# Low parts of four weights: a transfer that adds the weight to its negated upper part, in place of a subtraction on VectorE

## The chip, the cores and the metric

The kernel runs on one core of a Trainium2 chip. The metric is the device time of one execution in microseconds (us). The core's engines have separate instruction queues, each worked off in order: TensorE (PE: matmuls, with PEld its weight loads), VectorE (DVE), ScalarE (ACT), GpSimd (POOL) and SyncE (SP, which here only issues transfers). Each waits for the others by semaphores. Transfers run on 16 DMA engines, whoever issues them.

## The reference

A recurrence over time (4 batches, 8 heads, 768 steps, head size 48) gives the rows x of a gated network:

```
state = alpha[:, :, t, :, None] * state + k[t] (outer) v[t]
y[:, :, t] = q[t] @ state
x = y as 3072 rows of 384
h = x @ w_in            # 384 x 2048
g = h * tanh(log1p(exp(h)))
out = g @ w_out         # 2048 x 384
```

The weights come as 64-bit numbers, everything else as f32.

## The kernel before

**The work.** The recurrence is cut into 24 chunks of 64 steps by 2 pairs of batches; each becomes a few dozen small matmuls on PE (the turned keys, L724; products with the state and scores, L745 to L763; values and the update of the state, L783 to L809), with scans and products on DVE (L672 to L700). A chunk's output is 128 rows of x. The network goes in 100 *units*: a unit takes 2 or 4 chunks (256 or 512 rows) through one of 16 weight blocks f. A unit has an *up* (L1017, nine matmuls into a bank h), a chain on ACT and DVE (L1026, L1029, L1032, L1035 on ACT; the gate, L1044, on DVE; L1051 on ACT for g's upper part; L1054 on DVE for its lower part) and a *down* (L1089, three matmuls for each of its chunks). There are two banks h, so an up waits until the gate has read the bank of the unit two before.

**Two parts for every operand.** A product in full precision is made of three: upper by upper, upper by lower, lower by upper. So each weight block is split into an upper part `ws[:, 0, f]` and a lower part `ws[:, 1, f]`. The first two of every three matmuls use the upper part of the weight, the third the lower part.

**How a weight is made (`weight`, L401 on).** SP loads 768 KB into one of 2 `stage` buffers. DVE puts the bits together in one of 2 `lead` buffers in three steps (L428, L433, L438). ACT writes the upper part (L449). The lower part is `lead` minus the upper part, in one of three ways that the table `W_LOW` names per block: by PE and ACT (L467 to L471), by POOL (L477, two halves) or by DVE (L455):

```
    6: ('DVE', ''), 7: ('POOL', ''), 8: ('POOL', ''), 9: ('DVE', ''), 10: ('DVE', ''), 11: ('POOL', ''),
    12: ('POOL', ''), 13: ('POOL', ''), 14: ('DVE', ''), 15: ('POOL', ''),
```

So DVE makes the low parts of blocks 6, 9, 10 and 14. Below, w6 means block 6; unit n's buffers are t*n* and g*n*. Units 8 to 14 are the first seven wide ones and use w4 to w10 in turn.

**The order.** Every operation is a `Task` with an engine, a cost, a lateness, a due key, the tasks that it needs and the buffers that it uses. `Plan.order` plays these through in a model of the engines and issues them in the order that comes out, so an added or dearer task moves others on all engines. What runs on the chip is that fixed order, with waits for what each instruction needs.

Of the kernel before, what the change touches and what calls it, by code (L numbers as in the profile page):

```python
# [11 lines left out]
F32 = mybir.dt.float32  # L12
# [4 lines left out]
AF = mybir.ActivationFunctionType  # L17
ALU = mybir.AluOpType
# [103 lines left out]
class Plan:  # L122
# [13 lines left out]
    def add(  # L136
        self, engine, cost, late, key, emit, needs=(), uses=(), behind=(), port=False, size=0,
        sends=False, steps=0,
    ):
        t = Task(engine, cost, late, key, emit, port)  # L140
        t.size, t.sends, t.steps = size, t.sends or sends, steps
        t.needs, t.uses, t.behind = list(needs), list(uses), list(behind)
        for u in t.uses:
            u.left += 1
            u.key = min(u.key, key)
        self.tasks.append(t)
        return t
# [131 lines left out]
COST = {  # L279
    "load": (0.45, 2.0), "apart": (0.19, 0.32),  # L280
    "move": (0.63, 2.5), "store": (0.4, 3.0),
    "fill": (0.23, 0.28), "fill0": (0.44, 0.47),
    "off": (0.55, 0.75), "w off": (0.84, 1.08), "lead": (0.47, 0.58), "bits": (0.87, 0.98),
    "w hi": (0.745, 0.88), "w left": (0.42, 0.56), "w lo": (1.05, 1.2), "w lo2": (0.88, 1.0),
    "w check": (0.92, 1.2),
    "scan": (1.16, 1.27), "inverse": (0.09, 0.21), "mult": (0.6, 0.72), "check": (0.2, 0.34),
    "state": (0.48, 0.55), "state0": (0.5, 0.6), "mask": (0.65, 0.8),
# [22 lines left out]
def fast_path(ctx, tc, qka, v, w, out, good):  # L310
    nc = tc.nc
# [64 lines left out]
    add, last_col = plan.add, NSEG * (L + 1)  # L376

    def new(buffer, shape, name, pool=None, dtype=F32):
        buffer.tile = (pool or sb).tile(
            shape, dtype, tag=buffer.tag, name=name, bufs=plan.slots[buffer.tag]  # L380
        )
        return buffer.tile


    def in_bank(bank):
        return sums_at[int(bank.tag[1])] if bank.tag != "h" else h_at[bank.slot]
# [20 lines left out]
    ready_w, checked = {}, []  # L407

    def weight(f):
        key = weight_unit[f] - W_LEAD + W_SHIFT.get(f, 0.0)  # L410
        stage = plan.buffer("stage")

        def load():
            t = new(stage, [P, 2, DM, 2], f"ws{f}", dtype=I32)
            return nc.sync.dma_start(
                t.rearrange("p m c w -> p (m c w)"),
                w[f].rearrange("p m c -> p (m c)").bitcast(I32),
            )

        got = add(  # L420
            "SP", *COST["load"], max(key, FIRST_W + f) - 4, load, uses=[stage], size=786
        )
        lead = plan.buffer("lead")
        words = lambda z: stage.tile[:, :, :, z]

        def begin():
            new(lead, [P, 2, DM], f"w_lead{f}", dtype=I32)
            nc.vector.tensor_scalar(  # L428
                lead.tile, words(1), 3, 0x3FFFFFF8, ALU.logical_shift_left, ALU.bitwise_and
            )  # L430

        def signs():
            nc.vector.scalar_tensor_tensor(  # L433
                lead.tile, words(1), -0x40000000, lead.tile, ALU.bitwise_and, ALU.bitwise_or
            )

        def ends():
            nc.vector.scalar_tensor_tensor(  # L438
                lead.tile, words(0), 29, lead.tile, ALU.logical_shift_right, ALU.bitwise_or
            )  # L440

        bits = add("DVE", *COST["lead"], key, begin, [got], [stage, lead], port=True)
        bits = add("DVE", *COST["bits"], key + 0.01, signs, [bits], [stage, lead], port=True)
        bits = add("DVE", *COST["bits"], key + 0.02, ends, [bits], [stage, lead], port=True)
        both = lambda: lead.tile.bitcast(F32)
        hi, lo = ws[:, 0, f], ws[:, 1, f]

        def upper():
            nc.scalar.activation(hi, both(), AF.Copy)  # L449

        a = add("ACT", *COST["w hi"], key + 0.03, upper, [bits], [lead])
        how, tag = W_LOW[f]
        if how == "DVE":
            def lower():
                nc.vector.tensor_tensor(lo, both(), hi.bitcast(F32), ALU.subtract)  # L455

            b = add("DVE", *COST["w lo2"], key + 0.035, lower, [a], [lead], port=True)
            ready_w[f, 0] = ready_w[f, 1] = [a, b]
            return
        for m in range(2):  # L460
            k = key + 0.5 * m
            if how == "PE":
                bank = plan.buffer(tag)

                def off(bank=bank, m=m):
                    p = in_bank(bank)[:, :DM]
                    nc.tensor.matmul(p, ident, both()[:, m], start=True, stop=False)  # L467
                    nc.tensor.matmul(p, minus_ident, hi[:, m], start=False, stop=True)

                def left(bank=bank, m=m):  # L470
                    nc.scalar.activation(lo[:, m], in_bank(bank)[:, :DM], AF.Copy)  # L471

                t = add("PE", *COST["w off"], k + 0.04, off, [a], [lead, bank], steps=6)
                b = add("ACT", *COST["w left"], k + 0.05, left, [t], [bank])
            else:
                def lower(m=m):
                    nc.gpsimd.tensor_tensor(  # L477
                        lo[:, m], both()[:, m], hi[:, m].bitcast(F32), ALU.subtract
                    )

                b = add("POOL", *COST["w lo"], k + 0.04, lower, [a], [lead], port=True)
            ready_w[f, m] = [a, b]
# [692 lines left out]
    for f in range(NFF):  # L1175
        weight(f)
        weight_check(f)
# [285 lines left out]
```

## Time and profile before

| | |
|---|---|
| median of 3 runs | 498.51 us (498.22 to 499.92) |
| the profiled execution, its own time | 497.71 us |
| its span, first to last instruction | 496.0 us |
| PE busy | 484.6 us (98%) |
| ACT busy | 382.1 us (77%) |
| DVE busy | 323.1 us (65%) |
| POOL busy | 25.3 us (5%) |
| granted TensorE clock | 0.998 of 2.4 GHz |

The page of the profile has the busy time of each engine, the span in 40 slices and the chain of work that ended last. Views of the trace give the instructions in order of time, the waits (who waited for whom) and the transfers. Matmuls are pipelined, so the length of one contains the passage of others; the step from one group's start to the next is the price used below.

### The profile page before, as it was taken

How to read it: one execution, taken by the hardware profiler on the slowest of the kernel's cores; microseconds unless marked ns; L12 is line 12 of the kernel's file. 1: busy time of each engine (PE TensorE's matmuls, PEld its weight loads, DVE VectorE, ACT ScalarE, POOL GpSimd, SP SyncE). 2: the span in 40 equal slices, each digit the busy share in tenths (PEclk: the TensorE clock that was granted, in tenths of full speed). 3: DMA queues.
4: the chain of work that ended last, by engine and by line, in shares of the span. 5: the costliest groups of instructions: out<-in, count | busy, mean ns of one | idle time of the engine just before them, and what ended most of it. 6: DMA issues, size and time to landing. Idle time of an engine off the chain costs nothing.

```text
span 496.0 us, 12822 instructions
## 1 busy us (share of the span) xinstructions
PE 484.6 (98%) x5319; PEld 432.5 (87%) x5319; DVE 323.1 (65%) x522; ACT 382.1 (77%) x864; POOL 25.3 (5%) x27
## 2 busy tenths in 40 slices
PE   6999999999999999999999999999999999999995
PEld 4688889899899989999989899999989899999994
DVE  7999999999973694447867783863474343343333
ACT  3578786886788778857777897889789899997772
POOL 2003201413000000000000000000000000000000
PEclk9999999999999999999999999999999999999999
DMA  7877544606000250115152543603153412100001
GB/s 248 316 285 236 181 151 157 238 35 214 13 0 9 78 172 1 66 59 175 28 213 75 183 164 99 207 24 118 71 171 93 172 41 106 64 1 0 1 0 68
DMA packets 18926, 56.22 MB, mean 113 GB/s; under 512 B 3440, under 2 KB 11312, under 8 KB 18864
## 3 DMA queue, kind: packets, MB, share of 16 engines
q1 hardware_dynamic: 18592, 55.11, 32.5%
q8 instruction: 42, 0.69, 0.6%
q10 hardware_dynamic: 272, 0.26, 0.2%
q14 instruction: 20, 0.16, 0.1%
HBM read 48.87 MB, written 4.72 MB: 108 GB/s over the span
## 4 chain that ended last, share of the span: by engine, by line
PE 85%; DVE 9%; DMA 3%; issue 1%; ACT 1%; SPq 0%; DVEq 0%; ACTq 0%
PE sums_at L1089 39%; PE h_at L1017 37%; PE att_at L790 2%; PE att_at L752 2%; DVE w_lead L433 2%; PE h_at L763 2%; DMA ws<-in_wp_dram 1%; DVE w_lead L438 1%; PE att_at L724 1%; DMA qka<-in_qka_dram 1%; PE h_at L802 1%; DVE w_lead L428 1%; DVE t L1044 1%; DVE g L1054 1%; DVE rest L672 1%
## 5 line engine op out<-in xcount | busy, mean ns | idle before, releaser
L1089 PE MATMUL sums_at<-ws,g 128*128 128x384 f32 x1152 | 223.9, 340 | 0.1
L1017 PE MATMUL h_at<-xs,ws 128*128 128x512 f32 (+1 forms) x900 | 214.2, 384 | 0.2 <-DVE t L1044 0.2
L1089 PEld LDWEIGHTS sums_at<-ws,g 128*128 128x128 f32 x1152 | 202.4, 188 | 8.1 <-ACT ws L471 0.4
L1017 PEld LDWEIGHTS h_at<-xs,ws 128*128 128x128 f32 x900 | 163.3, 188 | 28.4 <-DVE t L1044 0.5
L1054 DVE SCALAR_TENSOR_TENSOR g<-t,g 128x512 fp32r<-128x512 f32 (+1 forms) x100 | 67.8, 679 | 124.2 <-ACT g L1051 123.9
L1026 ACT ACTIVATE t<-h_at 128x512 f32<-128x512 f32 (+1 forms) x100 | 58.0, 580 | 63.6 <-PE h_at L1017 60.8
L1051 ACT ACTIVATE g<-t 128x512 fp32r<-128x512 f32 (+1 forms) x100 | 60.3, 604 | 11.5 <-PE sums_at L1089 5.3
L1029 ACT ACTIVATE t<-t 128x512 f32<-128x512 f32 (+1 forms) x100 | 61.3, 613 | 2.3
L1032 ACT ACTIVATE t<-t 128x512 f32<-128x512 f32 (+1 forms) x100 | 61.2, 612 | 2.2
L1044 DVE SCALAR_TENSOR_TENSOR t<-t,h_at 128x512 f32<-128x512 f32 (+1 forms) x87 | 57.1, 657 | 8.3 <-ACT t L1035 8.2
L1035 ACT ACTIVATE t<-t 128x512 f32<-128x512 f32 (+1 forms) x100 | 60.4, 604 | 0.5
L672 DVE TENSOR_TENSOR_SCAN rest<-qka,behind 112x520 f32<-112x520 f32 x24 | 30.4, 1268 | 0.4 <-DMA qka<-in_qka_dram 0.2
L685 DVE TENSOR_TENSOR_SCAN qka<-qka,ahead 112x520 f32<-112x520 f32 x24 | 30.6, 1274 | 0.0
L477 POOL TENSOR_TENSOR ws<-w_lead,ws 128x384 fp32r<-128x384 f32 x14 | 22.1, 1598 | 98.3 <-ACT ws L449 98.3
L1026 ACT ACTIVATION_READ_ACCUMULATOR t<-h_at 128x1 f32 x100 | 19.4, 194 | 0.0
L1041 DVE COPY held<-h_at 128x512 f32<-128x512 f32 x13 | 9.0, 691 | 15.8 <-ACT t L1026 15.8
L831 ACT ACTIVATE xs<-att_at 112x384 fp32r<-112x384 f32 (+1 forms) x24 | 12.2, 513 | 6.2 <-PE att_at L809 3.4
L695 DVE TENSOR_TENSOR qka<-qka 112x512 f32<-112x512 f32 x24 | 16.4, 684 | 0.1
L681 DVE TENSOR_TENSOR qka<-qka,rest 112x512 f32<-112x512 f32 x24 | 15.8, 659 | 0.0
L433 DVE SCALAR_TENSOR_TENSOR w_lead<-ws,w_lead 128x768 int32<-128x768 int32 x16 | 15.7, 982 | 0.1
L438 DVE SCALAR_TENSOR_TENSOR w_lead<-ws,w_lead 128x768 int32<-128x768 int32 x16 | 15.3, 957 | 0.1
L449 ACT ACTIVATE ws<-w_lead 128x768 fp32r<-128x768 f32 x16 | 13.4, 839 | 2.3 <-DVE w_lead L438 2.2
(100 smaller groups left out, 366.7 us busy)
## 6 DMA issues: line engine op xcount, KB each, us to landing
qka<-in_qka_dram SPq DMA_DIRECT2D x22, 772.5 KB, 5.8
ws<-in_wp_dram SPq DMA_DIRECT2D x16, 768.0 KB, 4.5
wc<-in_wp_dram SPq DMA_DIRECT2D x16, 768.0 KB, 4.5
v<-in_vp_dram SPq DMA_DIRECT2D x24, 192.0 KB, 4.5
out_dram<-osb SPq DMA_DIRECT2D x15, 192.0 KB, 2.6
xs<-x SPq DMA_DIRECT2D x104, 16.0 KB, 1.8
out_dram<-part SPq DMA_DIRECT2D x8, 192.0 KB, 2.6
qka<-in_qka_dram SPq DMA_DIRECT2D x2, 260.5 KB, 4.4
```

The lines of the kernel that those rows point to most:

```text
L433: nc.vector.scalar_tensor_tensor(lead.tile, words(1), -0x40000000, lead.tile, ALU.bitwise_and, ALU.bitwise_or)
L672: nc.vector.tensor_tensor_scan(t[:, :0:-1], alpha()[:, :0:-1], behind[:, ::-1], 0.0, ALU.mult, ALU.max)
L685: nc.vector.tensor_tensor_scan(a, a, ahead, 0.0, ALU.mult, ALU.max)
L1017: nc.tensor.matmul(p[:, :N].rearrange("p (c t) -> p c t", c=nt), wi[:, z, f, s], x[:, :, s, a], start=m == 0, stop=m == len(passes) - 1,)
L1026: nc.scalar.activation(wide(t), wide(h), AF.Exp, accum_out=vchk[:, at : at + 1])
L1029: nc.scalar.activation(wide(t), wide(t), AF.Square, bias=1.0)
L1032: nc.scalar.activation(wide(t), wide(t), AF.Ln, bias=0.2, scale=0.2)
L1035: nc.scalar.activation(wide(t), wide(t), AF.Exp, scale=-1.0)
L1044: nc.vector.scalar_tensor_tensor(wide(y), wide(t), 2.5, wide(held), ALU.subtract, ALU.mult)
L1051: nc.scalar.activation(g.tile[:, 0, :N], wide(y), AF.Copy, scale=-0.4, accum_out=own)
L1054: nc.vector.scalar_tensor_tensor(g.tile[:, 1, :N], wide(y), -0.4, g.tile[:, 0, :N].bitcast(F32), ALU.mult, ALU.subtract,)
L1089: nc.tensor.matmul(o.tile, g.tile[:, a, j * C : (j + 1) * C], wo[:, z, f], start=begins and m == 0, stop=end and m == 2,)
```

## The change

For blocks 6, 9, 10 and 14 the subtraction on DVE goes. ACT, after the upper part, writes its negative into the place of the lower part (L455 in the new file), and POOL issues a transfer from `lead` to that place that adds what it brings to what is there (L458). PE's matmuls with the lower part wait for the transfer to land, and the `lead` buffer stays taken until then. In the plan the negation costs what the upper part costs, the transfer 1.0 on POOL with a result after 6.0, and neither its bytes nor its place among the transfers in flight are counted.

```diff
@@ -451,6 +451,17 @@
         a = add("ACT", *COST["w hi"], key + 0.03, upper, [bits], [lead])
         how, tag = W_LOW[f]
         if how == "DVE":
+            def negated():
+                nc.scalar.activation(lo, hi.bitcast(F32), AF.Copy, scale=-1.0)
+
+            def summed():
+                return nc.gpsimd.dma_start(lo, both(), accum_op=ALU.add)
+
+            b = add("ACT", *COST["w hi"], key + 0.035, negated, [a], [lead])
+            b = add("POOL", 1.0, 6.0, key + 0.04, summed, [b], [lead])
+            ready_w[f, 0] = ready_w[f, 1] = [a, b]
+            return
+        if how == "DVE":
             def lower():
                 nc.vector.tensor_tensor(lo, both(), hi.bitcast(F32), ALU.subtract)
```

Lines after L455 stand 11 higher in the new file (L1017 becomes L1028, L1089 becomes L1100). The instructions on PE are the same in number and kind. Their order is the same up to the down of unit 7, differs over some 400 rows, and is the same again from there to the end (996 of 1574 rows, which begin at about 210 us in the trace of before).

On PE, at the first place where the order differs, before (h_at0 and h_at1 are the two banks h; g8 is unit 8's result; qka6 and v6 belong to chunk 6):

```order
L1089 MATMUL sums_at2_108<-ws_103,g7_917 128x384 x3
L1017 MATMUL h_at0_111<-xs0_104,ws_103 128x512 x9
L1089 MATMUL sums_at3_109<-ws_103,g7_917 128x384 x3
L1089 MATMUL sums_at0_106<-ws_103,g8_1039 128x384 x3
L1089 MATMUL sums_at1_107<-ws_103,g8_1039 128x384 x3
L724 MATMUL att_at_110<-ident_69,qka6_647 128x112 x4
L1017 MATMUL h_at1_112<-xs0_104,ws_103 128x512 x9
L1089 MATMUL sums_at2_108<-ws_103,g8_1039 128x384 x3
```

and now:

```order
L1100 MATMUL sums_at2_108<-ws_103,g7_917 128x384 x3
L1100 MATMUL sums_at3_109<-ws_103,g7_917 128x384 x3
L1100 MATMUL sums_at0_106<-ws_103,g8_1027 128x384 x3
L1100 MATMUL sums_at1_107<-ws_103,g8_1027 128x384 x3
L1100 MATMUL sums_at2_108<-ws_103,g8_1027 128x384 x3
L735 MATMUL att_at_110<-ident_69,qka6_647 128x112 x4
L1100 MATMUL sums_at3_109<-ws_103,g8_1027 128x384 x3
L756 MATMUL att_at_110<-qka6_647,v_apart_96 64x64 x12
L763 MATMUL att_at_110<-qka6_647,state_91 48x64 x12
L774 MATMUL att_at_110<-qka6_647 64x64 x16
L1028 MATMUL h_at0_111<-xs0_104,ws_103 128x512 x9
```

The up into h_at0 is unit 10's, the first with w6. It stood ahead of unit 8's down and now stands behind it and behind the first half of chunk 6. In the same way unit 28's up, the first with w14, stood ahead of unit 26's down and now stands behind it.

On DVE, from the third step of w6's bits on, now (chunk 6's scan and products, g8, w8's bits and the first step of w9's):

```order
L438 SCALAR_TENSOR_TENSOR w_lead6_915<-ws6_711,w_lead6_915 128x768
L1055 SCALAR_TENSOR_TENSOR t8_953<-t8_953,h_at0_111 128x512
L688 RECIPROCAL ahead_85<-rest6_919 112x8
L692 TENSOR_TENSOR qka6_647<-qka6_647,rest6_919 112x512
L696 SCALAR_TENSOR_TENSOR qka6_647<-qka6_647,ahead_85 112x520
L711 TENSOR_TENSOR state_91<-state_91,rest6_919 112x384
L706 TENSOR_TENSOR qka6_647<-qka6_647 112x512
L1065 SCALAR_TENSOR_TENSOR g8_1027<-t8_953,g8_1027 128x512
...
L438 SCALAR_TENSOR_TENSOR w_lead8_1050<-ws8_823,w_lead8_1050 128x768
L428 TENSOR_SCALAR w_lead9_1133<-ws9_1014 128x768
```

The subtraction for w6 stood behind the product L692; now the scan L696 follows at once, and two further products of chunk 6 (L711, L706) have moved ahead of g8. The last row writes the `lead` buffer that w6 had, so it waits for w6's transfer.

On POOL, whose whole work after the first 4 us is this, now:

```order
L488 TENSOR_TENSOR ws_103<-w_lead7_698,ws_103 128x384 x2
L458 DMA ws_103<-w_lead6_915 128x768
L488 TENSOR_TENSOR ws_103<-w_lead8_1050,ws_103 128x384 x2
L458 DMA ws_103<-w_lead9_1133 128x768
L458 DMA ws_103<-w_lead10_1242 128x768
L488 TENSOR_TENSOR ws_103<-w_lead13_1346,ws_103 128x384 x2
...
L458 DMA ws_103<-w_lead14_1748 128x768
```

The four transfers (L458) are new; the subtractions of the POOL blocks keep their order around them.

## Rows read from the trace of the kernel before

**Rows 1.** The page, busy time of each engine over the span.

```profile
PE 484.6 (98%) x5319; PEld 432.5 (87%) x5319; DVE 323.1 (65%) x522; ACT 382.1 (77%) x864; POOL 25.3 (5%) x27
```

**Rows 2.** Waits of PE's weight loads, 60 to 210 us: total us, times, longest.

```profile
PEld h_at L1017 <- DVE t L1044: 0.5, 1, 0.5
```

**Rows 3.** Chain that ended last, 55 to 100 us: start, us, what.

```profile
87.05 0.83 DVE ws L455
...
95.70 2.34 PE h_at L1017 x9
```

**Rows 4.** PE in order of time, 62 to 92 us: start, us, work.

```profile
62.41 1.31 PE L1089 MATMUL sums_at<-ws,g 128*128 128x384 f32 x6
...
75.07 0.90 PE L809 MATMUL att_at<-state,ident 112*112 112x192 f32 x4
75.68 2.36 PE L1017 MATMUL h_at<-xs,ws 128*128 128x512 f32 x9
77.88 2.26 PE L1089 MATMUL sums_at<-ws,g 128*128 128x384 f32 x12
79.98 0.55 PE L724 MATMUL att_at<-ident,qka 112*128 112x112 f32 x4
80.29 2.37 PE L1089 MATMUL sums_at<-ws,g 128*128 128x384 f32 x12
...
84.65 0.58 PE L745 MATMUL att_at<-qka,v_apart 48*64 48x64 f32 x24
...
85.96 1.83 PE L1089 MATMUL sums_at<-ws,g 128*128 128x384 f32 x9
87.72 0.58 PE L783 MATMUL att_at<-probs,v_apart 64*64 64x64 f32 x24
...
88.92 2.37 PE L1017 MATMUL h_at<-xs,ws 128*128 128x512 f32 x9
91.13 0.68 PE L1089 MATMUL sums_at<-ws,g 128*128 128x384 f32 x3
```

**Rows 5.** DVE in order of time, 60 to 72 us: start, us, work.

```profile
60.80 0.68 DVE L1044 SCALAR_TENSOR_TENSOR t<-t,h_at 128x512 f32<-128x512 f32 x1
61.39 0.19 DVE L677 RECIPROCAL ahead<-rest 112x8 f32<-112x8 f32 x1
61.51 0.64 DVE L681 TENSOR_TENSOR qka<-qka,rest 112x512 f32<-112x512 f32 x1
62.07 0.94 DVE L455 TENSOR_TENSOR ws<-w_lead,ws 128x768 fp32r<-128x768 f32 x1
62.94 1.23 DVE L685 TENSOR_TENSOR_SCAN qka<-qka,ahead 112x520 f32<-112x520 f32 x1
64.29 0.69 DVE L1054 SCALAR_TENSOR_TENSOR g<-t,g 128x512 fp32r<-128x512 f32 x1
...
65.56 0.68 DVE L695 TENSOR_TENSOR qka<-qka 112x512 f32<-112x512 f32 x1
...
67.23 0.55 DVE L700 TENSOR_TENSOR state<-state,rest 112x384 f32<-112x384 f32 x1
67.69 0.56 DVE L428 TENSOR_SCALAR w_lead<-ws 128x768 int32<-128x768 int32 x1
...
70.23 0.95 DVE L438 SCALAR_TENSOR_TENSOR w_lead<-ws,w_lead 128x768 int32<-128x768 int32 x1
```

**Rows 6.** ACT in order of time, 60 to 66 us: start, us, work.

```profile
60.91 0.84 ACT L449 ACTIVATE ws<-w_lead 128x768 fp32r<-128x768 f32 x1 [0.54 <-DVE w_lead L438]
61.66 0.58 ACT L1026 ACTIVATE t<-h_at 128x512 f32<-128x512 f32 x1
62.13 0.19 ACT L1026 ACTIVATION_READ_ACCUMULATOR t<-h_at 128x1 f32 x1
```

**Rows 7.** POOL's subtractions: ns shortest/median/longest, first and last start.

```profile
L477 POOL TENSOR_TENSOR ws<-w_lead,ws x14: 1012/1184/4257, 45.0 to 123.3; 128x384 fp32r<-128x384 f32 x14
```

**Rows 8.** Transfers, 60 to 100 us: busy tenths (a digit per us); KB, us to landing.

```profile
DMA  7999810101007899740079300006999899500369
...
ws<-in_wp_dram SPq DMA_DIRECT2D x6, 768.0 KB, 4.5
...
xs<-x SPq DMA_DIRECT2D x5, 16.0 KB, 1.8
```

## The prediction

> **What bounds the kernel now.** I read the page first: PE is busy for 484.6 of 496.0 us and, its own weight loads aside, no other engine for more than 77% [rows 1]. Then PE's waits: from 60 to 210 us, where all of the change lies, the longest named wait is 0.5 us, for a gate on DVE [rows 2]. So PE is the bound, and an engine beside it can only cost time, or give back what PE now loses. But the chain of work says more: from 62 to 95 us it runs through DVE almost without a break, w10's subtraction in it (0.83 us at 87.05), and comes back to PE only at 95.70 [rows 3]. There DVE is as full as PE and is just in time. The reader is to see two things: PE has next to nothing to gain, and between 62 and 95 us its order hangs on when DVE, ACT and now a transfer deliver.
>
> PE's prices are steps from one group's start to the next [rows 4]: an up of nine 2.20 us (75.68 to 77.88); a down of three 0.525 (12 matmuls, 77.88 to 79.98); the turned keys 0.31 (79.98 to 80.29); the first half of a chunk 1.31 (84.65 to 85.96), the second 1.20 (87.72 to 88.92); the two state matmul pairs 0.61 (75.07 to 75.68). DVE's instructions start about 0.08 us before the one ahead ends, so a row counts 0.08 less than its length [rows 5].
>
> **Removed.** Four subtractions of 0.94 us on DVE [rows 5], 3.8 us together; three of them (w6, w9, w10) lie in the full stretch, w14's much later where DVE has gaps. None lies on PE. They are worth only what PE waits for DVE: the 0.5 us of [rows 2], of which I take 0.4 as regained.
>
> **Added on ACT.** Four negations, each priced as the upper part that it copies, 0.84 us [rows 6], less 0.1 overlap. ACT is not full, so their own 3 us hide; what counts is that each stands ahead of something. The one for w6 follows the exp that ended at 62.3 [rows 6] and ends at 63.1. Behind it stands g8's upper part, ready at 63.8 and so not late.
>
> **Added on POOL and the DMA engines.** No row shows a transfer that adds. It reads two operands of 384 KB, as many bytes as a weight load moves, which landed after 4.5 us [rows 8]; POOL must issue it, for which the nearest row is POOL's median subtraction, 1.2 us [rows 7]. I take 4.5 + 1.2 = 5.7 us from the negation's end to the landing. Low end: the smallest transfer, 1.8 us [rows 8], with POOL's shortest row, 1.0: 2.8. High end: two weight loads one after the other, 9.0, with 1.2: 10.2. I take the middle value since the bytes are those of the weight load. POOL itself is nearly idle, and its subtractions for w8 stand behind w6's issue by one such row only; the two halves for w8 are wanted at about 76 us and done by 75.
>
> **Moved: the order on PE, 62 to 92 us.** This I walk through, from the same start, 62.41 [rows 4].
>
> Unit 10, the first with w6, filled PE at 63.56 while g8 was still being made. Now the order has three downs there (62.41 + 1.6 = 64.0) and then g8's. Its third pass needs g8's lower part. On DVE that comes after scan, two products and itself: 62.07 + 1.15 + 0.47 + 0.60 + 0.69 = 64.98 [rows 5]. Two passes take PE to 64.33: **first gap 0.65**. Then one pass and three downs, 66.73; keys, 67.04; first half of chunk 6, 68.35; two passes of unit 10, 68.84. Here w6's transfer is wanted. It lands at 63.1 + 5.7 = 68.8: no wait, and no margin.
>
> Unit 10 ends at 70.55; second half, state and unit 11 at 74.6; two downs at 75.65. Unit 12 needs the bank that unit 10's gate frees. DVE, by ten rows after g8, ends w8's third step at 71.4 (it was 71.18 [rows 5]); then seven rows, L428, L677, L681, L433, L685, L438 and the gate, 0.56 + 0.19 + 0.64 + 0.95 + 1.23 + 0.95 + 0.68 less 0.56 overlap, 4.6: **second gap 0.4**, to 76.0. The first of these seven waits for w6's transfer, since it takes its `lead` buffer; at 68.8 that landed long before 71.4.
>
> Unit 12 ends at 78.2; keys, six downs and the first half of chunk 7 at 83.0; two passes of g11, 83.35. Its lower part is twelve DVE rows after the gate, 7.9 us: 83.9, **third gap 0.55**. Pass, down and two passes of unit 13: 85.1, where w9 is wanted; its negation ends five ACT rows after its upper part, at 79.1, so it lands at 84.8. Unit 13, second half, five downs and two passes: 91.1, where w10 is wanted. Its negation ends at 85.3, and it would land at 91.0; but from 88 to 94 us loads keep the DMA engines at 80% or more [rows 8], and sharing them costs it about 1.0, a choice between nothing and the 2.7 us by which a weight load lands later than the smallest transfer: **wait 0.9**. Without that wait unit 14 ends at 92.8. Before, the same work ended at 91.13 + 0.51 = 91.64 [rows 4].
>
> w14 stands apart. Unit 28, the first with it, now follows unit 26's down. Counted from the end of unit 26's up, ACT does the four steps of that chain, g25's upper part and a copy, then the negation, done at 4.0; landing at 9.7. PE first does unit 27 and fifteen downs, 2.2 + 7.9, and two passes, and wants it at 10.6: no wait, 0.9 to spare. From about 210 us the order on PE is that of before, and PE has been full there: what is lost by then stays lost.
>
> **The sum.** 92.8 - 91.64 = 1.2; w10's wait 0.9; regained at 95.70, -0.4: **+1.7 us**. On the profiled execution's own time, 497.71, that gives 499.4; the median of the runs stands 0.8 higher, at 498.51, and on it the sum gives **500.2 us**. A measurement of this kernel can tell 0.3% from no change, 1.5 us: the forecast lies just above that edge.
>
> **The rivals.**
>
> *The transfers land early.* At 2.8 us w10's wait goes and w6 and w9 have 3 us to spare: +0.8, 499.3, no change. For it: the engines are idle when w6's starts, with digits of 0 and 1 from 65 to 71 us [rows 8]. Against: a small plain copy already takes 1.8. The Trainium skill has a rule for this in "DMA: Bandwidth & Descriptors", section "Anatomy of one DMA — SWDGE (gpsimd) path": about 2.0 us plus bytes over 436 GB/s, which as an estimate is 2.9 us for 384 KB, half of what I take; no row of before shows a transfer from POOL. By that rule the time would be this rival's.
>
> *The transfers land late.* At 10.2 us w6 is 4.5 late; the second and third gap absorb about 1, and w9's and w10's windows give that back as new waits, so that about 1 us is lost per us late: 1.7 - 0.9 + 4.5 = +5.3, 503.8. It decides from 5.7 us on. DVE would then also stand, since w9's first step waits for the buffer from 71.4 on. For it: an operation on every element is more than any transfer of before does. Against: its bytes are only those of a weight load.
>
> *POOL's first use is dear.* Its first subtraction took 4.26 us against a median of 1.18 [rows 7]. If a first transfer costs the same 3.1 more, only w6 is late, and about 1 is absorbed: 1.7 + 2.1 = +3.8, 502.3.
>
> *DVE was the bound.* The chain of [rows 3] runs over DVE; freed of 2.8 us there, PE wins back its wait and the 1.1 us by which its steps from 62.41 to 91.64 exceed the work in them at the prices above: -1.5, 497.0. For it: the chain. Against: PE's named wait is 0.5, and the new order makes gaps of its own. It decides if the three gaps above don't appear, which needs g8, unit 10's gate and g11 each about 0.6 earlier.
>
> **How the numbers follow.** The forecast has 0.50; its own spread is +0.7 to +2.7, 0.22 of it under 1.5 us. Early landing 0.22; late landing 0.17; a dear first use 0.05; DVE as the bound 0.06. So faster by over 0.3%: 0.06; within: 0.22 + 0.22 = 0.44; slower: 0.28 + 0.17 + 0.05 = 0.50. The range goes from 497.8, short of the gain, to 504.3, past the late landing's 503.8.
>
> **What would show it.** Right: in the profile after, PE has gaps of about half a microsecond at 64, 76 and 83 us and one named for the transfer at 91; L455 on DVE is gone; four POOL transfers of 384 KB land about 4.5 us after issue; PE's last 280 us look as before, shifted by 1 to 2 us. Wrong: a transfer's landing under 4 or over 7 us; a wait of PE over 1 us for w6; a gap anywhere after 100 us that is not in the trace of before; a PE that is ahead of the old one at 92 us.

## The result, and the profile after

The changed kernel takes **503.79 us** (median of 3 runs, 503.26 to 504.35) against 498.51 before: a ratio of 1.0103, 95% interval 1.0084 to 1.0122, so 4.2 to 6.1 us slower. The forecast was 500.2 in a range of 497.8 to 504.3: the sign and the range held, and the size was three times the +1.7 us forecast. The profiled execution has a span of 502.1 us against 496.0.

From the page of the kernel after, in its order: busy time by engine, the new DMA queue, and the issues of the four transfers (KB each, median us to landing):

```profile
PE 488.1 (97%) x5319; PEld 432.9 (86%) x5319; DVE 319.6 (64%) x518; ACT 385.0 (77%) x868; POOL 28.0 (6%) x31
...
q0 software_dynamic: 576, 1.57, 1.7%
...
ws<-w_lead POOLq DMA_DIRECT2D x4, 384.0 KB, 5.3
```

Against [rows 1] DVE has lost 3.5 us and four instructions, ACT has gained 2.9 us and four, POOL four. Work went off DVE as the diff says. The landings are near where the forecast had them: counted from the end of the negation, w6's transfer landed after 5.5 us, w9's after 4.3, w14's after 5.7 (forecast 5.7 each), w10's after 7.6 (forecast 6.7). The transfers did roughly what was said of them, and still the loss is three times as large.

Waits of PE's weight loads and of PE from 60 to 210 us (total us, times, longest; rows of other engines are left out), where the longest before was the 0.5 us of [rows 2]:

```profile
PEld h_at L1028 <- DVE t L1055: 2.0, 3, 1.2
...
PEld h_at L1028 <- DMA ws<-w_lead: 1.5, 1, 1.5
PE h_at L1028 <- DVE t L1055: 1.2, 3, 0.8
PEld sums_at L1100 <- DVE g L1065: 1.1, 2, 0.7
...
PE h_at L1028 <- DMA ws<-w_lead: 1.0, 1, 1.0
PEld att_at L756 <- ACT ks L739: 1.0, 2, 0.6
...
PEld att_at L735 <- DVE xs L848: 0.7, 1, 0.7
```

Two of these seven lines, PEld's and PE's view of one wait, are for a transfer. The others are for DVE and ACT, and they are what the reader should look at: DVE has less to do than before, and PE waits for it more. PE in order of time (start, us, work, in brackets the idle time and what ended it) shows where:

```profile
66.25 1.51 PE L1100 MATMUL sums_at<-ws,g 128*128 128x384 f32 x7 [0.41 <-DVE g L1065]
...
77.97 2.34 PE L1028 MATMUL h_at<-xs,ws 128*128 128x512 f32 x9 [0.16 <-DVE t L1055]
...
84.17 0.58 PE L756 MATMUL att_at<-qka,v_apart 48*64 48x64 f32 x24 [0.33 <-ACT ks L739]
...
92.76 0.62 PE L1028 MATMUL h_at<-xs,ws 128*128 128x512 f32 x2
94.42 3.93 PE L1028 MATMUL h_at<-xs,ws 128*128 128x512 f32 x16 [1.04 <-DMA ws<-w_lead]
...
104.92 2.34 PE L1028 MATMUL h_at<-xs,ws 128*128 128x512 f32 x9 [0.83 <-DVE t L1055]
...
166.03 0.98 PE L735 MATMUL att_at<-ident,qka 112*128 112x112 f32 x8 [0.34 <-DVE xs L848]
...
188.95 2.33 PE L1028 MATMUL h_at<-xs,ws 128*128 128x512 f32 x9 [0.20 <-DVE t L1055]
```

Since a matmul's end is modelled, I count a **stall** from start to start: what the step between two matmuls is longer than the median step behind a matmul of that line and shape (only stalls over 0.15 us). And since the whole program is a row of 100 units, the starts of the same unit in two traces show where time is lost. Units between which the order differs don't compare; unit 9, units 24 to 27 and those from 41 on stand a steady distance apart, with the same work ahead of them in both:

| start of unit | before | after | behind | lost in the stage |
|---|---|---|---|---|
| 2 | 31.79 | 31.84 | 0.05 | |
| 3 (order as before) | 40.87 | 42.10 | 1.23 | 1.2 |
| 9 (order as before) | 59.29 | 60.53 | 1.24 | 0.0 |
| 27 | 146.14 | 151.13 | 4.99 | 3.75 |
| 43 | 221.96 | 228.28 | 6.32 | 1.33 |
| 99, the last | 479.86 | 486.18 | 6.32 | 0.0 |

The 1.2 us between units 2 and 3 stand ahead of the first negation and the first transfer; DVE's first step on a weight load, which waits for that load, began 0.9 us later there. The change's own loss in the traces is thus **5.08 us, all of it from 60 to 222 us**: 3.75 with w6, w9 and w10, and 1.33 with w14.

### The profile page after: what moved, and what is told of

It is laid out like the page before. It is cut to its first block, busy times and chain, and to the rows that moved or that the text cites. A ratio compares the mean times of both kernels' runs of the same rounds, so it can differ in the third digit from the quotient of the medians.

```text
span 502.1 us, 12838 instructions
## 1 busy us (share of the span) xinstructions
PE 488.1 (97%) x5319; PEld 432.9 (86%) x5319; DVE 319.6 (64%) x518; ACT 385.0 (77%) x868; POOL 28.0 (6%) x31
## 4 chain that ended last, share of the span: by engine, by line
PE 65%; DVE 0%; ACT 0%; issue 0%
PE sums_at L1100 31%; PE h_at L1028 29%; PE att_at L801 2%; PE att_at L763 2%; PE h_at L774 1%; PE h_at L813 1%; PE att_at L735 1%; DVE xs L848 0%; DVE t L1055 0%; ACT t L1037 0%; ACT t L1046 0%; DVE x L848 0%; ACT osb L1157 0%; PE att_at L1247 0%
## 5 line engine op out<-in xcount | busy, mean ns | idle before, releaser
L1100 PE MATMUL sums_at<-ws,g 128*128 128x384 f32 x1152 | 223.8, 340 | 0.5 <-DVE g L1065 0.4
L1028 PE MATMUL h_at<-xs,ws 128*128 128x512 f32 (+1 forms) x900 | 214.3, 384 | 2.2 <-DVE t L1055 1.2
L1100 PEld LDWEIGHTS sums_at<-ws,g 128*128 128x128 f32 x1152 | 202.3, 188 | 8.9 <-DVE g L1065 1.1
L1028 PEld LDWEIGHTS h_at<-xs,ws 128*128 128x128 f32 x900 | 163.1, 188 | 31.4 <-DVE t L1055 2.0
L1055 DVE SCALAR_TENSOR_TENSOR t<-t,h_at 128x512 f32<-128x512 f32 (+1 forms) x87 | 57.2, 658 | 10.8 <-ACT t L1046 10.5
L696 DVE TENSOR_TENSOR_SCAN qka<-qka,ahead 112x520 f32<-112x520 f32 x24 | 30.6, 1275 | 0.0
L706 DVE TENSOR_TENSOR qka<-qka 112x512 f32<-112x512 f32 x24 | 16.4, 684 | 0.5 <-DMA qka<-in_qka_dram 0.5
L692 DVE TENSOR_TENSOR qka<-qka,rest 112x512 f32<-112x512 f32 x24 | 16.4, 685 | 0.0
L801 PE MATMUL att_at<-probs,v 64*48 64x64 f32 (+1 forms) x720 | 15.2, 220 | 0.0
```

The costliest lines, as they stand in the source:

```text
L696: nc.vector.tensor_tensor_scan(a, a, ahead, 0.0, ALU.mult, ALU.max)
L801: nc.tensor.matmul(y[64 * a : 64 * a + wide, u, j], V()[own, h : h + wide], probs[slot][own, a, j], start=first and j == 0 and not direct ...
L1028: nc.tensor.matmul(p[:, :N].rearrange("p (c t) -> p c t", c=nt), wi[:, z, f, s], x[:, :, s, a], start=m == 0, stop=m == len(passes) - 1,)
L1055: nc.vector.scalar_tensor_tensor(wide(y), wide(t), 2.5, wide(held), ALU.subtract, ALU.mult)
L1100: nc.tensor.matmul(o.tile, g.tile[:, a, j * C : (j + 1) * C], wo[:, z, f], start=begins and m == 0, stop=end and m == 2,)
```

## The experiments

Two theories were put against each other. **Theory 1**: the landing of the transfers costs (PE's wait for w10, and the DMA engines that they share with the loads). **Theory 2**: the order costs. The plan reckons the four lower parts later, and so puts units and downs in another order, in which chains through DVE and ACT come too late for PE, whether or not a transfer is waited for. Each kernel has two readings: the ratio to the kernel before, run on the same chip, and, from its one trace, how far it is behind the old trace at the last matmul, less what it was behind at unit 9 ("lost from unit 9 on").

| kernel | ratio | 95% interval | lost from unit 9 on, us |
|---|---|---|---|
| the change | 1.0103 | 1.0084 to 1.0122 | 5.08 |
| kernel before, again | 0.9995 | 0.9972 to 1.0017 | 0.01 |
| w14 alone | 1.0014 | 0.9994 to 1.0034 | 1.72 |
| w6, w9, w10 alone | 1.0088 | 1.0055 to 1.0121 | 3.84 |
| new order, subtraction on DVE | 1.0082 | 1.0051 to 1.0113 | 5.15 |
| new order, no transfers | 1.0075 | 1.0054 to 1.0097 | 3.35 |
| plain copies | 1.0103 | 1.0080 to 1.0126 | 4.26 |
| old order with transfers | 1.0331 | 1.0300 to 1.0361 | 14.24 |
| plan's landing 6.5 for 6.0 | 1.0092 | 1.0058 to 1.0126 | 2.01 |
| other due times, first | 1.0053 | 1.0034 to 1.0071 | 2.28 (from unit 7) |
| other due times, second | 1.0086 | 1.0054 to 1.0117 | 2.65 (from unit 7) |
| plan that knows the DMA share | 1.0018 | 1.0001 to 1.0035 | 0.56 |

**The kernel before, once more** (no edit).

> The kernel before once more, for a second trace of it. The changed kernel was already 1.24 us behind at 41 us, before its first transfer and with the same order on TensorE; that came from a weight load that landed at 30.75 instead of 29.85 us. Theory 1 (chance: the loads of the first 40 us land differently from run to run): the fourth unit of this run starts anywhere between 40.8 and 42.2 us. Theory 2 (a transfer in the program delays the start): it starts at 40.9 as before, and in every kernel with a transfer at about 42.1. Time: ratio 1.000, within 0.002.

Its unit 3 starts at 42.51 us, 1.6 later than in the first trace and a little outside theory 1's 42.2, mostly by a stall of 1.15 us at 33.8 us, where PE waits for a state that stands on DVE behind the first step on that weight load, begun at 30.87 us instead of 29.85. No transfer is in this program. And the kernel with w14 alone, which has one, starts that unit at 40.87. So the start varies by itself, theory 2 of this expectation falls, and 1.2 of the 6.1 us between the two profiled spans are no work of the change. From unit 9 on the two traces of the kernel before agree to 0.01 us, which is what makes the last column above worth reading. It is one pair, though, and every other kernel has one trace.

**One part alone.** First w14, then the other three:

```diff
-        if how == "DVE":
+        if f == 14:
             def negated():
```

> Only w14 by transfer, the other three by VectorE as before. Theory 1 (my forecast: w14's transfer has 0.9 us to spare and its place costs nothing): 0.0 us, at most +0.5. Theory 2 (the planner puts units and downs in another order because the weight is late in its table, and that order has holes of its own whether or not the transfer is waited for): the trace of the change lost 1.35 us between units 27 and 41, so +1.3 to +2.1 us, with no TensorE wait on the transfer and small gaps on VectorE's or ScalarE's results between 150 and 200 us. If a transfer in the program delays the first 40 us, 1.2 us come on top.

The trace lost 1.72 us, 0.0 up to unit 27, and no wait for the transfer is in it: stalls of 0.20 (151.4 us, for g), 0.50 (161.0, for xs) and 0.78 (184.3, for a gate). The ratio, 1.0014, allows -0.3 to +1.7 us and can't decide alone. In the trace theory 2 holds: the transfer lands in time, and its order costs.

```diff
-        if how == "DVE":
+        if f in (6, 9, 10):
             def negated():
```

> w6, w9 and w10 by transfer, w14 by VectorE as before. Theory 1 (my forecast's holes at 64, 76 and 83 us, w10's wait, and 0.4 regained): +1.7 us, 1.2 to 2.7. Theory 2 (the planned order costs more than its holes up to 92 us; what the trace lost from 42 to 142 us was 3.75 us): +3.3 to +4 us. A delay of the start by the presence of a transfer would add 1.2 to either.

3.84 us in the trace, 4.4 by the ratio: theory 2's figure. With w14's 1.72 that makes 5.56 for 5.08, so the parts add up to within half a microsecond.

**The new order without the transfers**, in two ways. First with the old subtraction at the place of the transfer:

```diff
             def negated():
-                nc.scalar.activation(lo, hi.bitcast(F32), AF.Copy, scale=-1.0)
+                return None
 
             def summed():
-                return nc.gpsimd.dma_start(lo, both(), accum_op=ALU.add)
+                nc.vector.tensor_tensor(lo, both(), hi.bitcast(F32), ALU.subtract)
```

> The changed kernel's planned order kept, but where it issues a transfer VectorE does the old subtraction instead, and the negation is left out (no arithmetic is lost). Theory 1 (the landing of the transfers is what costs: w10's wait, the shared DMA engines): most of the loss goes, and what stays is the holes of the order, 0.8 to 1.5 us, VectorE's 2.8 us of extra work in the full stretch among it. Theory 2 (the order costs, not the transfer): the loss stays, +4 to +5.5 us, with TensorE's stalls at about the same units and the 0.9 to 1.2 us wait for w10 alone gone or replaced.

There is no transfer, no negation and nothing to land, and the loss is about that of the change: 5.15 us in the trace, and 1.0082 for 1.0103 with intervals that overlap. But this kernel has a cost of its own. PE in order of time:

```profile
67.30 1.49 PE L1100 MATMUL sums_at<-ws,g 128*128 128x384 f32 x7 [1.28 <-DVE g L1065]
...
79.02 2.34 PE L1028 MATMUL h_at<-xs,ws 128*128 128x512 f32 x9
...
84.82 0.58 PE L756 MATMUL att_at<-qka,v_apart 48*64 48x64 f32 x24
...
87.71 0.97 PE L1100 MATMUL sums_at<-ws,g 128*128 128x384 f32 x4 [0.81 <-DVE g L1065]
...
166.27 0.98 PE L735 MATMUL att_at<-ident,qka 112*128 112x112 f32 x8 [0.34 <-DVE xs L848]
...
189.19 2.34 PE L1028 MATMUL h_at<-xs,ws 128*128 128x512 f32 x9 [0.20 <-DVE t L1055]
```

The first idle time is 1.28 us instead of 0.41, because DVE has the subtraction ahead of g8 again; 0.81 us stands for g11 ahead of unit 13, behind w9's subtraction, and w10's wait is gone. The last two rows are the change's own, to the hundredth.

One stall of the change is missing here: the 0.49 us at 84.17, for the turned keys that ACT copies (L739). ACT of the change, in order of time (L455 is w9's negation):

```profile
80.08 0.84 ACT L455 ACTIVATE ws<-ws 128x768 fp32r<-128x768 f32 x1
...
83.64 0.47 ACT L739 COPY ks<-att_at 128x384 f32<-128x384 f32 x1
```

and of this kernel:

```profile
84.12 0.46 ACT L739 COPY ks<-att_at 128x384 f32<-128x384 f32 x1
```

In the change ACT has no idle time from the negation to the copy, which starts 5.67 us after unit 12's up (77.97). Here ACT's rows between are the same without the negation, the copy starts 5.10 us after that up (79.02), and PE, which takes it up at 84.82, doesn't wait. So this stall goes with w9's negation; no run takes the negations alone away.

Taking the landing away is thus not enough, but how the loss divides needs a kernel that leaves DVE alone:

```diff
             def summed():
-                return nc.gpsimd.dma_start(lo, both(), accum_op=ALU.add)
+                return None
```

> The changed kernel with its planned order and its negations, but the four transfers are left out, so the lower parts of w6, w9, w10 and w14 stay what the negation wrote (part of the computation is missing). What remains is the order with nothing late in it. Theory 1 (the transfers' landing and their load on the DMA engines cost): at most +0.8 us, my forecast's sum without w10's wait. Theory 2 (the order itself costs): the stalls at 66, 78 and 84 us and those between 156 and 189 us stay; w10's 1.2 us goes, and if the 1.0 us at unit 17 is an echo of that wait it goes too: +2.9 us; if it is not, +3.9. All counted from the tenth unit on, behind the start that varies by 1.6 us.

3.35 us stay, between theory 2's two values. PE in order of time:

```profile
65.18 1.49 PE L1100 MATMUL sums_at<-ws,g 128*128 128x384 f32 x7 [0.42 <-DVE g L1065]
...
76.90 2.34 PE L1028 MATMUL h_at<-xs,ws 128*128 128x512 f32 x9 [0.15 <-DVE t L1055]
...
83.11 0.58 PE L756 MATMUL att_at<-qka,v_apart 48*64 48x64 f32 x24 [0.34 <-ACT ks L739]
...
102.05 2.35 PE L1028 MATMUL h_at<-xs,ws 128*128 128x512 f32 x9 [0.31 <-DVE t L1055]
...
163.16 0.98 PE L735 MATMUL att_at<-ident,qka 112*128 112x112 f32 x8 [0.34 <-DVE xs L848]
...
186.07 2.35 PE L1028 MATMUL h_at<-xs,ws 128*128 128x512 f32 x9 [0.21 <-DVE t L1055]
```

These are the idle times of the change, row by row, but for w10's, and with 0.31 instead of 0.83 at unit 17. That divides the loss in the traces: **3.35 of 5.08 us stay without any transfer, 1.73 come with the transfers**. The 3.35 are the order with its four negations, the 0.49 us behind w9's among them; of the 1.73, 1.21 are w10's stall and 0.53 the longer stall at unit 17 (1.00 against 0.475).

**Plain copies**, for the price of adding:

```diff
             def summed():
-                return nc.gpsimd.dma_start(lo, both(), accum_op=ALU.add)
+                return nc.gpsimd.dma_start(lo, both())
```

> The changed kernel with plain copies in place of the adding transfers: the lower parts become the weight itself (so the result is another one), and the bytes written are the same. If the adding makes the landing long, the four land in about 3 us (the Trainium skill's rule in "DMA: Bandwidth & Descriptors", section "Anatomy of one DMA — SWDGE (gpsimd) path", gives an estimated 2.9) instead of 4.0 to 7.3, w10's wait of 1.2 us goes, and the time is that of the run without transfers. If the bytes, the issue on POOL and the sharing with loads make it, the landings stay within 1 us of those and so do w10's wait and the time, +5.3.

Each expectation is half right. The view of the line that issues the transfers, of the change and then of this kernel (POOL's ns shortest/median/longest; us from issue to landing):

```profile
L458 POOL DMA_DIRECT2D ws<-w_lead x4: 837/868/987, 64.6 to 153.7; - x4
...
DMA to landing us min/median/max: 4.0/5.3/7.3
```

```profile
L458 POOL DMA_DIRECT2D ws<-w_lead x4: 530/570/699, 63.2 to 151.4; - x4
...
DMA to landing us min/median/max: 2.7/4.7/6.5
```

By weight, from issue to landing: the adding transfers 5.15, 3.96, 7.28 and 5.35 us, the plain ones 6.43, 2.66, 6.47 and 2.88. Where no load was in flight for long (w9, w14) the plain copy takes 2.7 to 2.9. The Trainium skill's rule in "DMA: Bandwidth & Descriptors", section "Anatomy of one DMA — SWDGE (gpsimd) path", gives an estimate of 2.9 us for 384 KB, and these two copies agree with it. Adding costs 1.3 us more there at the least, and 0.3 us more on POOL. Where loads are in flight (w10's begins 1.45 us after one of 772 KB that itself takes 6.85 us; the plain w6 beside a weight load that takes 7.4), even the plain ones take over 6. So the long landings go with loads in flight, and adding makes about a microsecond of w10's. w10's stall went from 1.21 to 0.46 us, but the one at unit 17 stayed at 1.00, and the ratio did not move (1.0103). The trace lost 4.26 us, 0.8 less than the change; the trace is of the fastest of four executions (501.52 us; the others 502.79 to 504.20).

**The transfers in the order of before**: the plan sees the old subtraction, and in its place the negation and the transfer are issued.

```diff
             def lower():
-                nc.vector.tensor_tensor(lo, both(), hi.bitcast(F32), ALU.subtract)
+                nc.scalar.activation(lo, hi.bitcast(F32), AF.Copy, scale=-1.0)
+                return nc.gpsimd.dma_start(lo, both(), accum_op=ALU.add)
```

> The transfers in the order of before: where VectorE's subtraction stood, the negation and the transfer are issued, and the plan knows nothing of it. Both theories: TensorE wants w6 at 64.2, w9 at 83.1 and w10 at 89.6 us on before's clock, and the transfers, counted 5.7 us from the end of the negations at about 63.1, 82.1 and 87.9, land at 68.8, 87.8 and 93.6, w14 lands in time: waits of 4.6, 4.7 and 4.0, less the 0.4 regained, +13 us, all named for the transfer. If units that come later find their weights ready because the wait before gave time (the waits overlap), +6 to +9. What it is above the changed kernel is what the new order hid.

14.24 us in the trace. Waits of PE from 60 to 210 us:

```profile
PEld h_at L1018 <- DMA ws<-w_lead: 11.9, 3, 5.0
PE h_at L1018 <- DMA ws<-w_lead: 10.6, 3, 4.6
```

Three waits, with stalls of 4.74 (w6, forecast 4.6), 3.65 (w9, forecast 4.7) and 2.72 us (w10, forecast 4.0), together 11.1; none for w14. Nearly all of the rest is TensorE's clock, which the expected 13 us left out. Stretches of the trace (PE busy, instructions, granted clock, DMA share, GB/s):

```profile
64.60:69.60 5.00, 0.44 (x2) 0.98 0.77 204
69.60:73.00 3.40, 3.38 (x9) 0.53 0.06 15
73.00:85.00 12.00, 12.00 (x210) 1.00 0.43 149
...
89.00:93.80 4.80, 1.32 (x8) 0.94 0.57 133
93.80:97.30 3.50, 3.50 (x31) 0.59 0.71 227
97.30:105.00 7.70, 4.70 (x162) 1.00 0.70 189
105.00:108.00 3.00, 2.94 (x14) 1.00 0.63 246
```

After PE had stood for 4.7 and for 3.7 us, the granted clock was about half, the 1.2 GHz level, for some 3 us, in which seven steps lost 0.2 to 0.4 us each, 1.55 us together each time; after the wait of 2.7 us it stayed full. So the new order is no mere accident: it hid 9 of 14 us, and lost the other 5.

**Another order by one number.** The instructions stay, the plan reckons the landing half a microsecond later:

```diff
-            b = add("POOL", 1.0, 6.0, key + 0.04, summed, [b], [lead])
+            b = add("POOL", 1.0, 6.5, key + 0.04, summed, [b], [lead])
```

> The changed kernel with one number of the plan changed: it reckons a transfer's landing at 6.5 instead of 6.0 us. The instructions are the same, only the order that the planner makes of them differs. Theory 1 (landing and DMA sharing cost): the same transfers cost the same, +4 to +5.5 us. Theory 2 (what costs is the particular order that the planner falls into): the time moves by 1 to 3 us although the transfers are the same, with other gaps on TensorE at other places; w10's wait, which needs 7.3 us from issue, may stay.

This stays unclear. The profiled execution lost only 2.01 us, with w10's stall of 1.09 in it and no stall over 0.15 us anywhere after, against four in the change. But it was the fastest of six (499.74; the others 501.72 to 506.19), and by the median, 502.55, nothing is won. What the other five lost is in no trace.

**Due times.** If the order costs, then other due times should bring the time back with the same transfers. Two pairs of tables were tried with the change's plan, both found by searching for an early end of PE in the plan itself (the rows that were changed are those of w4 to w15 and of chunks 6 to 23; the weights' rows of the first):

```diff
 W_SHIFT = {
-    0: -30.0, 1: -2.75, 2: -3.75, 3: -1.75, 4: -3.5, 5: -9.25, 6: 0.25, 7: -4.75, 8: 2.5, 9: 2.75,
-    10: 2.25, 11: 7.0, 12: -6.25, 13: -7.75, 14: 30.25, 15: -1.75,
+    0: -30.0, 1: -2.75, 2: -3.75, 3: -1.75, 4: -3.25, 5: -6.75, 6: -2.5, 7: -6.0, 8: -1.25,
+    9: -0.75, 10: 0.25, 11: 8.25, 12: 6.75, 13: 0.75, 14: 6.25, 15: -6.25,
```

> The changed kernel with other numbers in the two tables of due times (the weights' from w4 on and the chunks' from 6 on), so that the planner, which knows of the four transfers, finds an order with fewer holes. Operations and transfers are the same. Theory 2 (the order costs): the time comes back to that of before, -0.5 to +1 us, and TensorE's stalls between 60 and 210 us add up to under 1 us. Theory 1 (transfers cost by landing and sharing, at least the 1.8 us that the run without them saved): +1.8 us or more, with waits for the transfers.

> A second such pair of tables, with w14's and the other weights' times elsewhere. The same two theories and numbers: -0.5 to +1 us if the order costs, +1.8 or more if the transfers do. It was made for landings of 6.0 us alone, so w10's, if it takes 7 again, may cost up to 1.2 us here and not in the other.

By time both fall on theory 1's side: 1.0053 and 1.0086 are +2.6 and +4.3 us, where it had +1.8 or more. The waits do not fit it: the first kernel waits for no transfer, the second 0.35 us for w10's. In the first, the stalls from 60 to 210 us do add up to 0.9 us, as theory 2 had it, and half the loss is back; but its trace has a stall of 1.42 us at 294.8 that waits for nothing the profile names, and the second has one of 1.42 at 82.5. Both tables also moved w4 and w5, and with them the order of the first 60 us: less work stands ahead of unit 9 than before, so the last column above counts these two from unit 7, where the work ahead is the same. So a third was made in which the first 60 us stay as they were and the plan knows more of a transfer:

```diff
+            if t.moves:
+                dma_free = max(at + 1.6, dma_free) + t.moves / DMA_RATE
+                t.late = dma_free + DMA_LAST - at
...
             b = add("POOL", 1.0, 6.0, key + 0.04, summed, [b], [lead])
+            b.moves = 590
...
-    0: -30.0, 1: -2.75, 2: -3.75, 3: -1.75, 4: -3.5, 5: -9.25, 6: 0.25, 7: -4.75, 8: 2.5, 9: 2.75,
-    10: 2.25, 11: 7.0, 12: -6.25, 13: -7.75, 14: 30.25, 15: -1.75,
+    0: -30.0, 1: -2.75, 2: -3.75, 3: -1.75, 4: -3.5, 5: -9.25, 6: -1.5, 7: -0.25, 8: -0.5,
+    9: -2.0, 10: 0.75, 11: 1.5, 12: 4.5, 13: 1.75, 14: 45.5, 15: 30.75,
```

> The changed kernel, in whose planner a transfer now takes its share of the DMA engines (it lands 1.6 us from issue plus 590 KB at the planner's own 285 KB a us plus 0.9 behind whatever is in flight, which gives the landings seen: 70.1 for 69.8, 85.8 for 85.2, 94.6 for 94.4 us), and in which the due times of w6 to w15 and of the chunks from 6 on are other numbers, so that every transfer lands before TensorE wants it. The first 60 us stand in the order of before. Theory 2 (what costs is the order): TensorE's stalls from 60 to 210 us add up to under 0.6 us, none of them for a transfer, and the time is within 0.5 us of before, -0.5 to +0.5. Theory 1 (the transfers cost something whatever the order, by the DMA engines that they share with loads and with the fetch of instructions, whose 1.4 us gaps cost both earlier tables): +1.5 us or more, with a gap for an instruction fetch or a late load.

**499.17 us, 1.0018** (1.0001 to 1.0035): 0.9 us behind before, a little outside theory 2's half microsecond and below theory 1's 1.5. The interval, 0.05 to 1.7 us, holds both figures, so the trace has to tell. Waits of PE from 60 to 210 us, the two longest:

```profile
PEld h_at L1033 <- DVE t L1060: 1.1, 1, 1.1
PE h_at L1033 <- DVE t L1060: 0.7, 1, 0.7
```

One stall of 0.91 us is left (at 64.7, for a gate) and one of 0.16, more than the 0.6 us that theory 2 had, and the old one of 0.4 at 95.7 is gone; the trace lost 0.56. No transfer is waited for, though w6's now takes 7.9 us to land: it is issued at 51.5 and has the time. Nor has the trace a stall of 1.4 us as with the two earlier tables, which theory 1 had expected. All four negations and transfers of the change are in this kernel, and by the ratios five sixths of the change's loss are not. The plan's account of a transfer and the tables changed together here, and the tables were not tried with the kernel before, so whether that one would gain by them too is not shown.

## Why the prediction came out as it did

**The bound** was read rightly: PE had next to nothing to gain. The stall of 0.4 us of [rows 2] is missing from the trace after, as forecast, but also from the run with the subtraction back on DVE, so it goes without the relief too. The relief shows between two runs of the new order, with the subtractions (5.15 lost) and with the negations alone (3.35): 1.8 us, which the transfers' 1.73 eat up. The rival "DVE was the bound" fell.

**The operations** were priced rightly, but not all of them hide. The four negations take 0.83 to 0.86 us (forecast 0.84). That on ACT "their own 3 us hide" failed for w9's: the forecast looked at what stands behind w6's alone, and w9's delays the turned keys on ACT, for which PE stalls 0.49 us at 84.17. The transfers landed 5.5, 4.3, 7.6 and 5.7 us after the negations (forecast 5.7, for w10 6.7), and "early landing" fell with the first of them. "Late landing" gave 503.8, the time that was measured, by 10.2 us and a wait for w6 that isn't there: a right number from a wrong mechanism. POOL's first transfer took 0.99 us there against 0.84 to 0.87 later, so "first use" fell too. That the time lies in the range is owed to the late landing, past which the upper end was put; the forecast's own spread ended at +2.7 us.

**The walk** through the new order found two of the three holes that it looked at. The third came out at nearly its size from another wait, which is luck. It missed the holes where it did not look:

| place | forecast, us | stall in the trace, us |
|---|---|---|
| first gap, g8's lower part | 0.65 | 0.57 |
| turned keys and first half of chunk 6 | none | 0.26, 0.19 |
| second gap, unit 12's bank | 0.4 | 0.32 |
| third gap, at 84 | 0.55, for g11 | 0.49, for the turned keys on ACT behind w9's negation |
| w6, w9 | no wait | no wait |
| w10 | 0.9 | 1.21 |
| unit 17's bank | none | 1.00 |
| regained at 95.70 | -0.4 | -0.39 |
| w14's stretch | none | 0.20, 0.50, 0.37 |

The stalls to unit 27 sum to 3.65 us net, and the units are 3.75 behind; those of w14's stretch to 1.07, of 1.33. **The step that failed** is the last line of the walk: "from about 210 us the order on PE is that of before", with nothing priced between 92 and 210 us. The order differs all that way, and only the first 30 us were walked. Unit 17's stall of 1.00 us lies there, and w14's whole stretch, where the forecast looked at the transfer alone (it wanted 10.6 us after unit 26's up and lands at 9.7, said the forecast; it landed at about 9.9) and set its place at nothing. Both are there without a transfer: the two kernels that have none stall 0.475 and 0.51 us at unit 17 and the same 0.20, 0.50 and 0.37 in w14's stretch. The other, smaller miss is w10's term, 0.9 for 1.21, and the two short holes of chunk 6. Together with three holes that came out 0.2 smaller and 0.4 of slack that the walk had credited to the new order, that makes 3.3 of the 3.4 us between the forecast's 1.7 and the trace's 5.08. Two of the forecast's own signs of being wrong came: a landing outside 4 to 7 us (from the issue, w9's 3.96 and w10's 7.28) and gaps after 100 us that the trace of before doesn't have.

What stands at unit 17 shows how such a hole is made. DVE of the kernel after, in order of time:

```profile
94.08 1.11 DVE L1065 SCALAR_TENSOR_TENSOR g<-t,g 128x512 fp32r<-128x512 f32 x1 [0.56 <-ACT g L1062]
...
99.63 0.69 DVE L1055 SCALAR_TENSOR_TENSOR t<-t,h_at 128x512 f32<-128x512 f32 x1 [0.98 <-ACT t L1046]
100.24 1.23 DVE L696 TENSOR_TENSOR_SCAN qka<-qka,ahead 112x520 f32<-112x520 f32 x1
101.41 1.43 DVE L1065 SCALAR_TENSOR_TENSOR g<-t,g 128x512 fp32r<-128x512 f32 x1
102.76 1.51 DVE L692 TENSOR_TENSOR qka<-qka,rest 112x512 f32<-112x512 f32 x1
104.19 0.67 DVE L1055 SCALAR_TENSOR_TENSOR t<-t,h_at 128x512 f32<-128x512 f32 x1
```

and POOL, in order of time:

```profile
100.93 2.78 POOL L488 TENSOR_TENSOR ws<-w_lead,ws 128x384 fp32r<-128x384 f32 x2 [6.29 <-ACT ws L449]
```

w10's wait leaves ACT and so DVE without work (0.98 us idle; the 0.56 before it are in the run without transfers too); then the gate of L1055 that frees unit 17's bank stands behind two operations that take 1.43 and 1.51 us beside POOL's subtraction, where the same lines took 0.69 and 0.64 in [rows 5]. In the traces of before and of the change these two lines take over 0.8 us six times, each time beside a POOL subtraction. PE waits 1.00. DVE of the run without transfers, at the same place:

```profile
99.30 0.67 DVE L1065 SCALAR_TENSOR_TENSOR g<-t,g 128x512 fp32r<-128x512 f32 x1
99.89 1.51 DVE L692 TENSOR_TENSOR qka<-qka,rest 112x512 f32<-112x512 f32 x1
```

Only the second is long there, and the stall is half, 0.475. With plain copies both are long again, 1.43 and 1.51, and the stall is 1.00, though w10's wait is only 0.46. So half of this stall goes with the first operation's 0.76 us more, and not with the length of w10's wait: where w10 is waited for, POOL's subtraction begins 0.69 us behind the scan of L696, and 0.44 in the run without transfers. That the other half is the second operation's is argued from these rows; no run takes POOL's subtraction away.

**Left open**: what the five slower runs of the 6.5 us plan lost; what the order alone costs, without w9's negation; and the two stalls of 1.42 us. The profile has a DMA queue for instructions, and in both traces a packet of 16 KB on it ended 1.5 us before PE went on, with loads on the engines just before. A late fetch of instructions would explain that, but no run takes it apart.

## What to carry to other kernels

When a change alters a number in a planner whose tables were fitted to the old numbers, price the order and not only the operation: walk the new order up to the place where it meets the old one again, and run once with the new order and the operation left out. Here that run, with the negations still in it, gave two thirds of the loss. And before such a change is given up as slow, fit the due times again with the operation's true landing in the plan: the same four transfers came with a loss of 5 us in one order and of 0.9 (0.05 to 1.7) in another. And follow every added operation on its own engine to the next thing that the bounding engine wants from there: here one negation of 0.84 us stood ahead of a copy that PE waited for. What the change freed on DVE only paid for what PE waited through the transfers.

## What the runs showed of the hardware

Of the 28 adding transfers of 384 KB from POOL's queue in these traces, half landed 3.9 to 4.7 us after their issue. Seven took 4.8 to 5.4 us, six of them beside weight loads and one (5.35) with nothing else in flight; one took 6.1, and six took 7.2 to 8.3 us, all beside loads of 768 or 772 KB. Of the four plain copies two landed after 2.7 and 2.9 us, and two beside such loads after 6.4 and 6.5. An adding transfer held POOL for 0.83 to 0.99 us, a plain one for 0.53 to 0.70. Small transfers land later beside one: the first three 16 KB transfers of xs behind w6's landed after 2.8 to 3.2 us, against 1.8 [rows 8] and against 2.0 to 2.2 in the run without transfers. A two-input DVE operation of 512 columns took up to 1.51 us beside a POOL subtraction, against 0.64 and 0.69 in [rows 5]. And TensorE's granted clock fell to its lower level behind waits of 3.7 and 4.7 us and did not behind one of 2.7.
